# A fused attention and MLP kernel on one core: one decay moved ahead of two load issues, one weight load cut in two, four chunks' loads issued sooner and four stores later

## The chip, the core and the metric

The kernel runs on one core of a Trainium2 chip. The core has a matrix engine (TensorE, PE in the profile; its weight loads are listed as PEld), a vector engine (VectorE, DVE), a scalar engine (ScalarE, ACT), a general engine (GpSimd, POOL) and a queue engine that only issues transfers (SyncE, SP). Each runs its own list of instructions in order, and they meet through semaphores. Transfers between the device memory and the on-chip memory (DMA) are done by 16 DMA engines that all issuing engines share. In this kernel POOL issues all loads, which change float32 to bfloat16 on the way, and SP issues the stores and the transposing copies inside the on-chip memory.

The metric is device microseconds of one launch, as a median of several runs.

## The reference

Two stages follow each other. The first is a linear attention with decay, over 4 batches, 8 heads, 768 positions and head width 64, in blocks of 64 positions:

```python
for b in range(nb):
    qb, kb, vb = (q[:, :, sl], k[:, :, sl], v[:, :, sl])
    intra = einsum('bhic,bhjc->bhij', qb, kb) * Dmask
    intra = einsum('bhij,bhjd->bhid', intra, vb)
    inter = einsum('bhid,bhde->bhie', qb * lam_pow, kv_state)
    out[:, :, sl] = intra + inter
    kv_state = lam_block * kv_state + einsum('bhsd,bhse->bhde', kb * rev_pow, vb)
```

The second takes the 3072 tokens of width 512 that come out, and computes `gelu(x @ w_in) @ w_out` with an inner width of 2048 and the exact gelu.

## The kernel before, in words

**Tiling.** Positions go in chunks of 128 (two blocks of 64). Chunk n belongs to group n // 4 and batch n % 4, so a group is the same 128 positions of all four batches, 512 tokens, and there are 6 groups and 24 chunks. For each group the attention makes a tile x of 128 x 4 x 512, and the MLP of the group (`mlp`, L417 and on) follows. Its first product runs in 16 blocks of 128 inner columns (named a, b, m or l with the block's number; the gelu on ACT follows each), its second in 16 pieces p0 to p15. In group 0 piece p4k+i is the k-th quarter of w_out for tokens of batch i; in group 1 and later p4i+k is the k-th quarter for batch i.

**What a visit is.** While PE runs the MLP of one group it makes, between named blocks, the attention of the next. `visit(f, d)` (L335) gives PE the scores of chunk d (q times k) and its states (kv_ps: keys times decayed V), and between them the outputs of chunk f. It comes as some 32 matmul pairs of 64 x 64 that PE issues about 30 ns apart. Of a visit's pairs for d, the first eight are scores, the next four the states of the chunk's first block, and the last four those of its second block.

**What a chunk needs first.** Its k and q (two loads of 128 KB, L71), both transposed (`kqT`; by PE for chunks 0 to 7, from chunk 8 on by two transposing DMAs on SP, L245 and L246, asked for by `request`); its V with the decay (`vd`, `decay_v`, L266, one POOL multiplication); and its keys in a by-block arrangement (`k2`, `by_block`, L248), four copies of 64 x 256, of which two are made by POOL (by VectorE for chunks 4 and 7) and two by ACT or DVE. V comes for a whole group in four loads of 128 KB (`load_blocks`, L91).

**What sets the order.** It is written out by hand. `run_blocks` runs the blocks of an MLP and calls, ahead of the named ones, the steps in a table: the one after `run_blocks(mlp(0, 2)` for group 0 and `plan_of(g)` (L613) for the later ones. Each step only adds instructions to the ends of the engines' lists, so a step's name says when it stands in the program, and each engine works through its own list as its waits allow. `values(n)` is the decay and POOL's two key copies of chunk n, `keys(n)` the other two key copies, `fetch(n, m)` the loads of chunks n and m, with V of a group behind its first chunk.

**The loads at the start.** One call (L141) issues q, k and V of group 0, w_in, w_out, and k and q of chunks 4 to 7 with group 1's V. `i8-12` is blocks 8 to 12 of w_in in two DMAs (one for each half of the partitions), each 256 KB in bfloat16. The landings of POOL's loads are told by eight semaphores used in turn, so a load's issue waits until the load eight places before it has landed.

```python
    ask("k0 q0 k1 q1 k2 q2 k3 q3 v0 v2 i0-2 i2-4 i4-6 i6-8 i8-12 i12-16 "
        "o0-4 k4 q4 o4-8 V1 o8-12 k5 q5 o12-16 k6 q6 k7 q7")
```

**Behind them on POOL**, from `ahead_of_group_1` (L560): vd 4, vd 5, k8, the two key copies of chunk 5, q8, vd 6, the first quarter of group 2's V, vd 7, the second quarter, the key copies of chunk 6, the other two quarters, k9, q9. `visit(None, 4)` stands ahead of p8 of group 0, `visit(4, 5)` ahead of p11, `visit(5, 6)` ahead of p15. The third quarter of w_out (o8-12) is first read by p8.

**SP's list** holds the requests and the stores. The four outputs of group 0 are not stored when they are made: `store` (L451) keeps them in `held`, and `store_held` (L400) stores them at m0 of group 2's MLP. Output buffers (o_sb) come from nine in turn, so the tenth one waits for the first one's store. SP's transfers, too, have eight semaphores in turn.

Of the kernel before, what the change touches and what calls it, by code (L numbers as in the profile page):

```python
# [15 lines left out]
def kernel(  # L16
# [12 lines left out]
    B, H, S, D = q.shape  # L29
# [38 lines left out]
    def load(n, name):  # L68
        g, b = n // B, n % B
        t = raw[n, name] = qkv_pool.tile([128, H, D], BF16, tag=name, name=f"{name}_t", bufs=10)  # L70
        nc.gpsimd.dma_start(t, dram[name][b, :, g * C:(g + 1) * C, :].rearrange("h si d -> si h d"))  # L71
# [3 lines left out]
    def load_pairs(n, name):  # L75
        if (n, "kq") not in raw:
            raw[n, "kq"] = qkv_pool.tile([128, H, 2, D], BF16, tag="kq", name="kq_t", bufs=B)
        t = raw[n, "kq"][half("kq".index(name))]
        src = dram[name][n, :, :C, :].rearrange("h (p j) d -> p h (j d)", j=2)
        nc.gpsimd.dma_start(t.rearrange("p h j d -> p h (j d)"), src)  # L80

    def load_parity(n):

        t = qkv_pool.tile([128, 2 * H, D], BF16, tag="v", name="v_t", bufs=2)
        src = v[n:n + 2, :, :C, :].rearrange("b h (p j) d -> j p (b h) d", j=2)
        for j in range(2):
            nc.gpsimd.dma_start(t[half(j)], src[j])
        for i in range(2):
            raw[n + i, "v"] = t[:, i * H:(i + 1) * H, :]

    def load_blocks(g):  # L91

        t = raw["group", g] = qkv_pool.tile([128, 2, B * HP, D], BF16, tag="vg", name="vg_t", bufs=3)
        src = v.rearrange("b (hp hi) s d -> hi s (b hp) d", hi=2)
        for u in range(2):
            for hi in range(2):
                s = g * C + u * L
                nc.gpsimd.dma_start(t[half(hi), u], src[hi, s:s + L])  # L98
                yield
# [23 lines left out]
    def ask(items):  # L123

        for item in items.split():
            name, at = item[0], item[1:]
            if name in "kqv":
                n = int(at)
                if name == "v":
                    load_parity(n)  # L130
                elif n < B:
                    load_pairs(n, name)
                else:
                    load(n, name)
            elif name == "V":
                for _ in load_blocks(int(at)):
                    pass
            else:
                (load_w_in if name == "i" else load_w_out)(*(int(x) for x in at.split("-")))

    ask("k0 q0 k1 q1 k2 q2 k3 q3 v0 v2 i0-2 i2-4 i4-6 i6-8 i8-12 i12-16 "  # L141
        "o0-4 k4 q4 o4-8 V1 o8-12 k5 q5 o12-16 k6 q6 k7 q7")

    idle = consts.tile([128, 512], BF16)
    nc.vector.memset(idle, 0.0)  # L145
# [65 lines left out]
    def begin(n):  # L211
        c = live[n] = Chunk()
        c.n, c.g, c.b = n, n // B, n % B
        if c.g:
            c.q, c.k = (raw.pop((n, name)) for name in "qk")
        else:
            c.kq = raw.pop((n, "kq"))
        c.v = of_group(n) if c.g else raw.pop((n, "v"))
        c.kqT = work_pool.tile([128, 2, HP, C], BF16, tag="kqT", name="kqT", bufs=6)
        c.kT, c.qT = c.kqT[:, 0], c.kqT[:, 1]  # L220
        return c
# [22 lines left out]
    def dma_transposes(c):  # L244
        nc.sync.dma_start_transpose(out=c.kT, in_=c.k.rearrange("p h d -> p (h d)"))  # L245
        nc.sync.dma_start_transpose(out=c.qT, in_=c.q.rearrange("p h d -> p (h d)"))  # L246
# [16 lines left out]
    def of_group(n):  # L263
        return raw["group", n // B][:, :, n % B * HP:(n % B + 1) * HP, :]

    def decay_v(n):  # L266
        vd[n] = work_pool.tile([128, 2, HP, D], BF16, tag="vd", name="vd", bufs=6)
        nc.gpsimd.tensor_mul(vd[n], of_group(n), lam_vb)  # L268
# [131 lines left out]
    def store_held(some):  # L400
        for r, w, o_sb in held[some]:
            nc.sync.dma_start(out[r:r + C, w], o_sb)
# [147 lines left out]
    def request(*ns):  # L550
        for n in ns:
            dma_transposes(live[n])

    def same(n, eng):
        by_block(live[n], eng, None)
# [3 lines left out]

    def ahead_of_group_1():  # L560

        for n in range(B, 2 * B):
            begin(n)
        decay_v(4)
        decay_v(5)
        ask("k8")
        same(5, nc.gpsimd)
        ask("q8")
        decay_v(6)
        v_of_2 = load_blocks(2)  # L570
        next(v_of_2)
        decay_v(7)
        next(v_of_2)
        same(6, nc.gpsimd)
        for _ in v_of_2:
            pass
        ask("k9 q9")
        begin(8)
        begin(9)
# [17 lines left out]
    def values(n):  # L597
        decay_v(n)
        by_block(live[n], nc.gpsimd, None)

    def keys(n):
        by_block(live[n], None, nc.vector)

    def fetch(*ns):
        ns = [n for n in ns if n < NG * B]
        for n in ns:
            ask(f"k{n} q{n}")
            if n % B == 0 and n > 2 * B:
                ask(f"V{n // B}")
        for n in ns:  # L610
            begin(n)

    def plan_of(g):  # L613
        if g == 1:
            n = 2 * B
            return {
                "a0": [lambda: values(n), lambda: request(n + 1)],
                "a2": [lambda: visit(n - 2, n - 1, first=True)],
                "b2": [lambda: fetch(n + 2, n + 3)],
                "m5": [lambda: keys(n), lambda: request(n + 2, n + 3)],  # L620
                "m8": [lambda: values(n + 1), lambda: values(n + 2)],
                "m12": [lambda: fetch(n + 4, n + 5), lambda: request(n + 4, n + 5)],
                "m14": [lambda: visit(n - 1, n, first=True)],
                "l4": [lambda: values(n + 3), lambda: keys(n + 1)],
                "p1": [lambda: visit(n, n + 1)],
                "p2": [lambda: keys(n + 2), lambda: keys(n + 3)],
                "p5": [lambda: values(n + 4), lambda: fetch(n + 6, n + 7), lambda: values(n + 5)],
                "p7": [lambda: request(n + 6, n + 7)],
                "p8": [lambda: visit(n + 1, n + 2)],
                "p9": [lambda: keys(n + 4)],  # L630
                "p12": [lambda: visit(n + 2, n + 3)],
                "p13": [lambda: fetch(n + 8, n + 9)],
                "p15": [lambda: visit(n + 3, n + 4)],
            }
        if g == NG - 1:
            return {}
        n = (g + 1) * B
        if g == 2:
            return {
                "m0": [lambda: store_held(slice(0, B))],  # L640
                "m2": [lambda: keys(n + 1)],
                "m7": [lambda: visit(n, n + 1)],
                "m8": [lambda: values(n + 2), lambda: request(n + 4, n + 5)],
                "m10": [lambda: keys(n + 2), lambda: values(n + 3)],
                "m13": [lambda: keys(n + 3)],
                "m15": [lambda: visits([n + 1], [n + 2, n + 3], ["mo1"])],
                "p0": [lambda: fetch(n + 6, n + 7), lambda: values(n + 4)],
                "p2": [lambda: request(n + 6, n + 7), lambda: values(n + 5)],
                "p8": [lambda: keys(n + 4), lambda: keys(n + 5)],
                "p12": [lambda: visits([n + 2, n + 3], [n + 4, n + 5], ["mh", "mh"]), lambda: values(n + 6)],  # L650
            }

        def each(act, *ns):
            for n in ns:
                if n < NG * B:
                    act(n)

        return {
            "m0": [lambda: fetch(n + 4, n + 5), lambda: values(n + 3)],
            "m4": [lambda: keys(n + 2), lambda: keys(n + 3)],  # L660
            "m8": [lambda: each(request, n + 4, n + 5)],
            "m14": [lambda: visits([n, n + 1], [n + 2, n + 3], ["mo0", "mo1"]), lambda: each(values, n + 4)],
            "p0": [lambda: fetch(n + 6, n + 7), lambda: each(values, n + 5)],
            "p4": [lambda: each(request, n + 6, n + 7)],
            "p8": [lambda: each(keys, n + 4, n + 5)],
            "p12": [lambda: visits([n + 2, n + 3], [n + 4, n + 5], ["mh", "mh"]), lambda: each(values, n + 6)],
        }

    for g in range(1, NG):
        if g + 1 < NG:  # L670
            alloc_x(g + 1)
        run_blocks(mlp(g, 4, NK2) if g == 1 else mlp(g), plan_of(g))
# [29 lines left out]
```

## Time and profile before

| | us |
|---|---|
| timed runs | 210.36, 211.28, 212.76; median 211.28 |
| the profiled execution's own time | 210.23 |
| its span, first to last instruction | 208.2 |
| TensorE busy | 196.4 (94%) |
| GpSimd busy | 106.3 (51%) |
| VectorE, ScalarE busy | 88.7, 86.4 |
| DMA engines busy | over 0.9 of the span's first 29 of 40 slices, the first apart; little after |

All positions in time below are microseconds from the start of the span. Around the span lie 2.0 us more in the profiled execution's own time. In the list of an engine's instructions a line gives the start, the duration, engine, line of the source, operation and tiles, and in brackets the idle time before it and what ended that. "Landing" is the time from a DMA's issue to the semaphore that tells of its end. A wait is put down to what came last.

### The profile page before, as it was taken

To read this page: it belongs to the slowest core of one execution; us is meant where nothing else is said; L and a number is where in the kernel's file an instruction comes from. 1 tells how busy PE (TensorE), PEld (TensorE's weight loads), DVE (VectorE), ACT (ScalarE), POOL (GpSimd) and SP (SyncE) were. 2 spreads that over 40 slices of the span, in tenths; PEclk is the share of its full clock that TensorE was granted. 3 is DMA by queue.
4 is the path that set the end of the run, shared out by engine and by line. 5 is a ranking of instruction groups with operands and counts; after the bars stand their busy time and mean duration, and the time that the engine had idled before them with its cause. 6 is when DMAs were issued, how large, how long until landed. Compare 5 with 4: busy or idle time off the path is not lost.

```text
span 208.2 us, 5534 instructions
## 1 busy us (share of the span) xinstructions
PE 196.4 (94%) x2382; PEld 103.8 (50%) x2410; DVE 88.7 (43%) x188; ACT 86.4 (42%) x157; POOL 106.3 (51%) x150
## 2 busy tenths in 40 slices
PE   7789999799999999999998999999999999999992
PEld 4545345356758445445444445445445445444461
DVE  3869505167708669644934902946103202000000
ACT  5386561038675211556111465311565211665120
POOL 8979656699299949999649705950000000000000
PEclk9999999999999999999999999999999999999999
DMA  6999999999999999999999999994100021100121
GB/s 58 153 170 184 200 187 176 184 155 102 113 89 122 112 152 108 180 146 196 273 139 172 124 264 70 118 158 133 50 3 3 3 98 54 50 0 0 50 100 56
DMA packets 97337, 24.49 MB, mean 118 GB/s; under 512 B 88992, under 2 KB 94368, under 8 KB 97312
## 3 DMA queue, kind: packets, MB, share of 16 engines
q0 software_dynamic: 76160, 13.64, 89.4%
q1 hardware_dynamic: 21152, 10.50, 27.8%
q8 instruction: 19, 0.31, 0.7%
q14 instruction: 6, 0.05, 0.1%
HBM read 27.27 MB, written 6.29 MB: 161 GB/s over the span
## 4 chain that ended last, share of the span: by engine, by line
PE 44%; DMA 30%; POOL 22%; issue 2%; ACT 0%; POOLq 0%
PE h_ps L427 20%; PE o_ps L466 20%; DMA vg_t<-in_v_dram 12%; DMA q_t<-in_q_dram 8%; POOL vd L268 5%; DMA w_in_t<-in_moe_w_in_dram 4%; POOL q_t L71 3%; POOL vg_t L98 3%; DMA v_t<-in_v_dram 3%; POOL k_t L71 3%; POOL kq_t L80 3%; POOL k L255 3%; DMA kqT<-q_t 2%; POOL w_in_t L118 2%; PE o_ps L477 2%
## 5 line engine op out<-in xcount | busy, mean ns | idle before, releaser
L427 PE MATMUL h_ps<-x_t,w_in_t 128*128 128x512 bf16 (+3 forms) x399 | 81.9, 358 | 1.3 <-DMA w_in_t<-in_moe_w_in_dram 0.8
L466 PE MATMUL o_ps<-w_out_t,g_t 128*128 128x512 bf16 x352 | 80.9, 379 | 1.1 <-issue 0.5
L436 ACT ACTIVATE g_t<-h_ps 128x512 bf16<-128x512 f32 (+1 forms) x96 | 55.1, 580 | 32.0 <-PE h_ps L427 32.0
L427 PEld LDWEIGHTS <-w_in_t 128*128 128x128 bf16 x408 | 38.6, 98 | 41.4 <-issue 2.8
L466 PEld LDWEIGHTS <-g_t 128*128 128x128 bf16 x368 | 35.0, 98 | 40.3
L325 DVE TENSOR_TENSOR x_t<-o_ps,lam_o 128x512 bf16<-128x512 f32 x24 | 15.9, 688 | 60.8 <-PE o_ps L333 60.8
L455 ACT COPY o_sb<-o_ps 128x512 f32<-128x512 f32 (+1 forms) x25 | 14.2, 569 | 65.5 <-PE o_ps L466 60.1
L268 POOL TENSOR_TENSOR vd<-vg_t,lam_v 128x512 bf16<-128x512 bf16 x20 | 21.2, 1064 | 18.8 <-DMA vg_t<-in_v_dram 17.8
L71 POOL DMA_DIRECT2D q_t<-in_q_dram x20 | 18.1, 904 | 1.6 <-DMA vg_t<-in_v_dram 1.5
L71 POOL DMA_DIRECT2D k_t<-in_k_dram x20 | 18.2, 908 | 0.3 <-issue 0.2
L98 POOL DMA_DIRECT2D vg_t<-in_v_dram x20 | 16.4, 835 | 2.2 <-DMA w_in_t<-in_moe_w_in_dram 2.2
L255 POOL COPY k<-k_t 64x256 bf16<-64x256 bf16 x36 | 14.6, 405 | 3.6 <-DMA k_t<-in_k_dram 2.6
L279 DVE TENSOR_TENSOR sm<-sc_ps,dmask 128x512 bf16<-128x512 f32 x20 | 13.2, 681 | 5.4 <-PE sc_ps L333 5.4
L259 DVE COPY k<-k_t 64x256 bf16<-64x256 bf16 x34 | 13.1, 386 | 1.3 <-DMA k_t<-in_k_dram 0.8
L333 PEld LDWEIGHTS <-kqT 64*64 64x64 bf16 (+1 forms) x352 | 7.6, 107 | 7.5 <-issue 5.6
L333 PE MATMUL sc_ps<-kqT 64*64 64x64 bf16 (+1 forms) x352 | 10.2, 197 | 1.1 <-DMA kqT<-q_t 0.7
L333 PE MATMUL kv_ps<-vd,k 64*64 64x64 bf16 x288 | 8.0, 193 | 1.4 <-POOL vd L268 1.4
L504 PE MATMUL idle_ps<-idle 128*128 128x256 bf16 (+1 forms) x31 | 7.7, 391 | 1.3 <-DVE idle L145 1.2
L333 PE MATMUL o_ps<-sm,vg_t 64*64 64x64 bf16 x320 | 8.5, 193 | 0.0
L304 DVE TENSOR_TENSOR state<-t,lam_c 128x256 bf16<-128x256 f32 x16 | 8.1, 508 | 0.6
L118 POOL DMA_DIRECT2D w_in_t<-in_moe_w_in_dram x12 | 7.5, 667 | 1.2 <-DMA v_t<-in_v_dram 1.2
L298 DVE CAST mid<-t 128x256 bf16<-128x256 f32 x13 | 7.8, 597 | 0.4
(72 smaller groups left out, 132.2 us busy)
## 6 DMA issues: line engine op xcount, KB each, us to landing
out_dram<-o_sb SPq DMA_DIRECT2D x23, 256.0 KB, 4.8
k_t<-in_k_dram POOLq DMA_DIRECT2D x20, 128.0 KB, 7.1
q_t<-in_q_dram POOLq DMA_DIRECT2D x20, 128.0 KB, 7.2
vg_t<-in_v_dram POOLq DMA_DIRECT2D x20, 128.0 KB, 7.2
w_out_t<-in_moe_w_out_dram POOLq DMA_DIRECT2D x4, 512.0 KB, 11.2
w_in_t<-in_moe_w_in_dram POOLq DMA_DIRECT2D x8, 128.0 KB, 5.4
w_in_t<-in_moe_w_in_dram POOLq DMA_DIRECT2D x4, 256.0 KB, 7.4
kq_t<-in_k_dram POOLq DMA_DIRECT2D x4, 128.0 KB, 4.0
```

The source lines that it names most:

```text
L71: nc.gpsimd.dma_start(t, dram[name][b, :, g * C:(g + 1) * C, :].rearrange("h si d -> si h d"))
L98: nc.gpsimd.dma_start(t[half(hi), u], src[hi, s:s + L])
L255: same.tensor_copy(c.k2[half(hi), hi], k_r[half(hi), :, hi, :])
L259: copy(c.k2[half(hi), 1 - hi], k_r[half(1 - hi), :, hi, :])
L268: nc.gpsimd.tensor_mul(vd[n], of_group(n), lam_vb)
L279: nc.vector.tensor_mul(c.sm, c.sc, dmask)
L325: nc.vector.tensor_mul(xT[c.g][:, :, c.b * C:(c.b + 1) * C], c.o, lam_o)
L333: nc.tensor.matmul(out_, lhsT, rhs, start=start, stop=True, skip_group_check=True)
L427: nc.tensor.matmul(hs[kf][:, lo:up], w_in_t[:, ki, kf * 128:(kf + 1) * 128], x_t[:, ki, lo:up], start=(ki == 0 and lo == 0), stop=(ki == N ...
L436: nc.scalar.activation(g_t[:, kf, :up], hs[kf][:, :up], ACT.Gelu)
L455: nc.scalar.copy(o_sb, ps_)
L466: nc.tensor.matmul(om[io], g_t[:, kf, io * C:(io + 1) * C], w_out_t[:, kf, :], start=(kf == 0), stop=(kf == NK2 - 1))
```

## The change

There are four edits.

1. w_in's blocks 8 to 12 come in two loads of two blocks (`i8-10 i10-12`), so as four DMAs of 128 KB instead of two of 256 KB.
2. k7 and q7 leave the first list of loads. They are issued in `ahead_of_group_1`, k7 between the decays of chunks 4 and 5 and q7 behind the decay of chunk 5.
3. In group 1's MLP, the loads of chunks 14 and 15 stand ahead of the decay and key copies of chunk 12 instead of behind them, and the loads of chunks 16 and 17, with group 4's V, stand ahead of p11 instead of p13.
4. In group 2's MLP, the transposes of chunks 16 and 17 are asked for at m0 ahead of group 0's stores, instead of at m8 behind them.

On PE, VectorE and ScalarE the instructions and their order are the same in both kernels. POOL has two more load issues, and POOL and SP have the moved ones in other places.

```diff
-    ask("k0 q0 k1 q1 k2 q2 k3 q3 v0 v2 i0-2 i2-4 i4-6 i6-8 i8-12 i12-16 "
-        "o0-4 k4 q4 o4-8 V1 o8-12 k5 q5 o12-16 k6 q6 k7 q7")
+    ask("k0 q0 k1 q1 k2 q2 k3 q3 v0 v2 i0-2 i2-4 i4-6 i6-8 i8-10 i10-12 i12-16 "
+        "o0-4 k4 q4 o4-8 V1 o8-12 k5 q5 o12-16 k6 q6")
...
     def ahead_of_group_1():
 
+        decay_v(4)
+        ask("k7")
+        decay_v(5)
+        ask("q7")
         for n in range(B, 2 * B):
             begin(n)
-        decay_v(4)
-        decay_v(5)
         ask("k8")
         same(5, nc.gpsimd)
         ask("q8")
...
-                "p5": [lambda: values(n + 4), lambda: fetch(n + 6, n + 7), lambda: values(n + 5)],
+                "p5": [lambda: fetch(n + 6, n + 7), lambda: values(n + 4), lambda: values(n + 5)],
...
-                "p13": [lambda: fetch(n + 8, n + 9)],
+                "p11": [lambda: fetch(n + 8, n + 9)],
...
-                "m0": [lambda: store_held(slice(0, B))],
+                "m0": [lambda: request(n + 4, n + 5), lambda: store_held(slice(0, B))],
...
-                "m8": [lambda: values(n + 2), lambda: request(n + 4, n + 5)],
+                "m8": [lambda: values(n + 2)],
```

## The prediction

> **What bounds it now.** I read the busy shares first, then who TensorE (PE) waited for, then the order on GpSimd (POOL) and SyncE (SP) around those waits, and last the chain of waits. The page's first two lines
>
> ```profile
> span 208.2 us, 5534 instructions
> PE 196.4 (94%) x2382; PEld 103.8 (50%) x2410; DVE 88.7 (43%) x188; ACT 86.4 (42%) x157; POOL 106.3 (51%) x150
> ```
>
> and of the waits of PE's own (total us, times, longest us):
>
> ```profile
> PE kv_ps L333 <- POOL vd L268: 1.4, 1, 1.4
> ...
> PE h_ps L427 <- DMA w_in_t<-in_moe_w_in_dram: 0.8, 2, 0.4
> PE sc_ps L333 <- DMA kqT<-q_t: 0.7, 1, 0.7
> ```
>
> PE is busy for 94% at a granted clock of 1.0 in every slice, so no work can get faster; only waits can go. PE, DVE and ACT run the same instructions in the same order in both kernels; only POOL and SP differ. The change touches three waits: 0.40 us at 24.16 (the 0.8 is two waits; the other, at 16.67, is for blocks 0-2), 1.45 us at 41.12, 0.74 us at 112.00. Together 2.59 us, 1.2% of the span: the most it can win. What counts is what is late next, so I look at the stretch of POOL around the longest:
>
> ```profile
> 36.73 0.87 POOL L71 DMA_DIRECT2D k_t<-in_k_dram  x1 [0.18 <-issue]
> 39.09 0.87 POOL L71 DMA_DIRECT2D q_t<-in_q_dram  x1 [1.48 <-DMA vg_t<-in_v_dram]
> 40.03 2.04 POOL L268 TENSOR_TENSOR vd<-vg_t,lam_v 128x512 bf16<-128x512 bf16 x2
> 42.02 0.91 POOL L71 DMA_DIRECT2D k_t<-in_k_dram  x1
> 42.93 0.87 POOL L255 COPY k<-k_t 64x256 bf16<-64x256 bf16 x2
> ...
> 48.41 0.87 POOL L255 COPY k<-k_t 64x256 bf16<-64x256 bf16 x2
> ```
>
> Each load that POOL issues waits until the eighth load before it has landed. k7's issue (36.73) stands in the idle time before the last part of group 1's V lands (38.81, in the chain below); q7's stands right behind that landing, then the decays of chunks 4 and 5 (vd, 2.04 us for two), k8's issue, the two key copies of chunk 5, and so on without a gap to 52.6. From 39.09 on this queue is the path: whatever is put into it shifts all behind it.
>
> ```profile
> 26.87 11.94 DMA vg_t<-in_v_dram
> ...
> 90.85 16.94 DMA q_t<-in_q_dram
> ```
>
> These are pieces of the chain of waits (start, us): V's last part, then chunk 17's q, 16.94 us to land. Its transpose, issued at 107.81 and 4.15 us long, ends the 0.74 us wait at 112.00.
>
> **The change, part by part.**
>
> *w_in's blocks 8-12 in two loads.* Two more issues on POOL, 0.61 us each (the row of seven at 14.53 took 4.31). They are covered by POOL's later waits for landings (0.86, 1.07, 0.31, 1.71 us, from 22.2 on). In the trace the 256-column loads land 0.67 us apart, the 512-column ones 1.28 us, so four small ones take 2.68 us where two large took 2.56: +0.1 us for every later landing. PE comes to block 8 at 23.76 and now needs the first pair alone. That pair should land near 21.9 (20.60, the last small one's landing, + 2 x 0.67), and block 10 is reached at 25.5 with its pair at 23.3: **-0.40 us**. Blocks 12-16 land at 26.7, PE is there at 27.2.
>
> *Chunk 4's decay ahead of k7 and q7.* V's last part lands at 38.81 + 0.1, POOL starts 0.28 us later (as at 39.09): vd 4 runs 39.1-40.15 instead of 40.03-41.07. But PE's next need is the third quarter of w_out, issued at 29.39, 11.3 us to landing: 40.66, now 40.75. PE's part of kv (0.35 us) ends near 40.5, so w_out ends the stall, near 40.85, where before PE went on at 41.49: **-0.64 us, the 0.40 contained in it**, for PE arrives at either wait.
>
> *What this costs on POOL.* Behind the V landing stood one issue (q7) ahead of k8; now two do (k7, q7), because k7 has left the idle time. So everything from k8 on is one issue, 0.87 us, later, plus the 0.1. No queue hides it. The second copy of chunk 5's keys, needed by the fifth kv pair of the visit that PE starts at 44.63, ends at 44.75 instead of 43.80; PE would use it at 45.03 - 0.64 = 44.4 and so waits 0.35 us: 0.3 us of gain is left. The second copy of chunk 6's keys ends at 49.28 before (48.41 + 0.87) and at **50.2** after. PE uses it in the visit that starts at 49.31:
>
> ```profile
> 49.58 0.20 PE L333 MATMUL kv_ps<-vd,k 64*64 64x64 bf16 x2
> ...
> 49.71 0.20 PE L333 MATMUL kv_ps<-vd,k 64*64 64x64 bf16 x2
> ```
>
> These are the first kv pair and the fifth, which reads that copy. The slack before was 49.71 - 49.28 = 0.43 us; 0.95 us of delay takes it and 0.5 us more. PE leaves this visit **0.5 us later than before**, and the whole early gain is gone: -0.64 becomes +0.5. The size depends on V's landing alone: 0.9 us sooner would save all of it, 1 us later costs 1 us more.
>
> *Group 1.* POOL's next wait is for group 2's V (vd at 56.68 after 4.05 us idle). It covers part of the 0.95; I keep 0.3 us of shift (bounds 0 and 0.95). PE's visits there have several us of slack, except one: chunk 12's transposes, whose q is issued by SP at 73.27 and lands 8.2 us later, at 81.43, while PE starts that visit at 82.64. With PE 0.5 later the slack is 1.7 us; 0.3 is used.
>
> *Loads of chunks 14-17 sooner.* Chunks 14 and 15: four issues, 3.6 us, now ahead of chunk 12's decay (77.50) and in the 2.94 us that POOL idled for V there, so vd 12 and its copies end at 80.1, not 79.4; PE wants them at 82.9: nothing. Chunks 16 and 17 follow chunk 13's copies on POOL in both kernels (the move from p13 to p11 passes nothing there), but that queue has lost its idle time: they come about 2.9 us sooner (q17 at 88.0, not 90.85). But the four loads of 14 and 15 now run while chunk 12's transposes do. Bounds: 0 and 3.5 us (four landings 0.87 apart, as loads land at 45 to 50 us). I take 0.5, within the slack, since loads already in the queue (k13, q13) are those that it meets first. The Trainium skill (DMA: Bandwidth & Descriptors, Queues, rings and completion order) says that each DMA engine goes round-robin over its queues packet by packet; by that, the transposes would keep half of the turns and this wait would be 0; no view parts the two queues in time, so the trace does not decide it. The 8.2 us against the shortest landing of a transpose, 2.4 us, show how much a full load queue can cost in this trace, so I keep the upper end.
>
> *Group 0's stores behind the requests of 16 and 17.* SP before:
>
> ```profile
> 89.36 1.20 SPq L246 DMA_TRANSPOSE kqT<-q_t  x1
> 90.65 1.63 SPq L459 DMA_DIRECT2D out_dram<-o_sb  x3
> 92.33 2.07 SPq L402 DMA_DIRECT2D out_dram<-o_sb  x4
> 98.11 1.25 SPq L245 DMA_TRANSPOSE kqT<-k_t  x1
> ```
>
> Seven stores of 256 KB went out in 3.8 us, and q17, issued at 90.85 among them, took 16.94 us. Now three go ahead, and q17 has left 2.9 us sooner. At about 9 us it lands near 97, its transpose near 103 (4 to 8 us), 8 us ahead of PE: **-0.74 us**. The held stores wait behind it on SP until about 98 and land by 105; behind them stand the requests of 18 and 19, needed at 128. Their buffers are needed again at 107.25 (group 2's second o_sb copy of nine buffers): 2 us of slack, and PE has the other bank for 3.5 us more. Also chunk 15's transposes, which landed at 98.03 for a visit at 98.09, now have some us to spare.
>
> **Sum.** +0.5 (chunk 6's copy, early gains included) - 0.74 = **-0.25 us** on the profiled execution: 210.23 to 209.98 us. That execution is below all three timed runs (210.36, 211.28, 212.76; median 1.05 above it). What the slower ones lose is in no view; the least slack (0.06 us at 98.09, none at 112.00) lies where the change gives some, so I leave half of the 1.05 in: **210.5 us**, all cases below with the same 0.5.
>
> **Rivals.**
> *Early gain kept* (V lands sooner, or POOL's shift meets other idle time): -0.64 - 0.74 = -1.4, 209.35 us. For it: the key copies of 5 and 6 miss by only 0.3 and 0.5 us. Against: POOL has no idle time between 39.09 and 52.6. Chance 0.27; all three waits gone (-2.59, 208.15) is its end, against w_out's landing.
> *Slower: chunk 12's transposes pushed back* by the four loads issued at 74.6-78.2. Place: PE's visit at 82.6; it decides once the landing moves by over 1.7 us. At the upper end, 81.43 + 0.3 + 3.5 = 85.2 against 83.1: 2.1 us, -0.25 + 2.1 = +1.85, 212.6 us. For it: 8.2 us to land already. Against: k13 and q13 are ahead of them. Chance 0.18.
> *The late q17 stays late* (three stores and the transposes of 14 and 15 still stand around it): +0.5 alone, 211.2 us. Against it: 8 us of slack. Chance 0.1.
> Forecast: 0.45.
>
> **The numbers.** Within 1% is about what a measurement here can tell from no change (2.1 us, the spread of the three runs being 2.4). Forecast and the third rival lie within it; the first reaches over 1% only near its end, the second only with slow runs. Faster 0.2, same 0.67, slower 0.13. The range takes in the first rival (209.35, less 0.35 for part of its end) and most of the second: 209.0 to 212.4.
>
> **What would show it.** PE's waits after: none for w_in at block 8; kv for vd 4 at about 0.9 us and ended near 40.2, then a short one for w_out; new waits for POOL's key copy of 0.35 us at the visit of 5 and some 0.8 us at that of 6; none for kqT at the visit of 16 and 17. The first visit in group 1 starts 0.5 us later than 52.23. q17 lands within 10 us. I am wrong if there is no wait for POOL's copies, or if PE waits for chunk 12's transposes.

## The result and the profile after

The changed kernel is faster by about half a per cent: over 20 runs of each, a median of 209.12 us against 210.35 us, and a ratio of 0.9943 with a 95% interval of 0.992 to 0.9966. Slow executions, of which the only profiled one is that of e6_stores below (its granted clock was 0.5 for 3.4 us), are left out of every ratio and of every comparison of traces. The profiled execution took 209.00 us, with a span of 207.0 us, against 210.23 and 208.2. The forecast was 210.5 us and -0.25 us on the profiled execution; -1.23 us came. The sign is right and the size is not, so the question is which term carries the rest. Both medians lie 0.12 us above their profiled executions.

The page's first two lines and the list of PE's waits, of the kernel after:

```profile
span 207.0 us, 5564 instructions
PE 199.3 (96%) x2410; PEld 104.2 (50%) x2410; DVE 84.7 (41%) x188; ACT 86.5 (42%) x157; POOL 107.2 (52%) x152
```

```profile
PE t_ps L230 <- DMA kq_t<-in_k_dram: 1.6, 1, 1.6
PE idle_ps L504 <- DVE idle L145: 1.2, 1, 1.2
PE kv_ps L333 <- POOL k L255: 0.3, 1, 0.3
PE h_ps L427 <- DVE x_t L325: 0.2, 1, 0.2
```

PE's work is the same; its busy time is higher because the profile before lacks 28 matmul records (2382 of 2410). All three waits that the change aimed at are gone, also the one for chunk 4's decay, of which 0.9 us were to stay. The 1.6 us at 7.8 us lie in the start, which the change does not touch, among the transposes of the first chunks; PE reached group 0's MLP at 16.45 (16.67 before). The forecast new wait is there: PE waits for a key copy of POOL. It is larger than the list says, because half of it stands inside a matmul's duration. PE's order of instructions in that visit (start, us; in brackets the idle time before):

```profile
48.23 0.22 PE L333 MATMUL kv_ps<-vd,k 64*64 64x64 bf16 x2 [0.30 <-POOL k L255]
...
48.38 0.52 PE L333 MATMUL kv_ps<-vd,k 64*64 64x64 bf16 x2
48.69 0.22 PE L333 MATMUL o_ps<-kqT,mid 64*64 64x64 bf16 x2
```

The first kv pair waits for the first copy and the fifth, at 48.38, for the second: 0.52 us where others take 0.20. The visit lasts from 47.48 to 49.00, 1.5 us, where it took 0.7 before. POOL in the same stretch:

```profile
37.62 1.04 POOL L268 TENSOR_TENSOR vd<-vg_t,lam_v 128x512 bf16<-128x512 bf16 x1 [1.63 <-DMA vg_t<-in_v_dram]
38.60 0.91 POOL L71 DMA_DIRECT2D k_t<-in_k_dram  x1
39.53 1.06 POOL L268 TENSOR_TENSOR vd<-vg_t,lam_v 128x512 bf16<-128x512 bf16 x1
40.52 0.92 POOL L71 DMA_DIRECT2D q_t<-in_q_dram  x1
41.43 0.88 POOL L71 DMA_DIRECT2D k_t<-in_k_dram  x1
42.30 0.87 POOL L255 COPY k<-k_t 64x256 bf16<-64x256 bf16 x2
...
47.77 0.87 POOL L255 COPY k<-k_t 64x256 bf16<-64x256 bf16 x2
```

k7's issue stands behind V's landing, as foreseen, but V landed earlier than foreseen. The chain of waits has it (start, us):

```profile
19.22 7.42 DMA w_in_t<-in_moe_w_in_dram
...
26.93 10.52 DMA vg_t<-in_v_dram
```

V's last part landed at 37.44, not at 38.81. From the same load of w_in to this landing it took 10.8 us, against 12.2 in the profile before. PE began the first visit of group 1 at 51.22, 1.0 us sooner than before, where 0.5 us later had been forecast. Of this, 0.55 us is there when chunk 4's visit begins (38.69 against 39.24), mostly by the earlier start of the MLP and the missing wait at block 8; the rest comes behind V's landing. From the first visit of group 1 to the last matmul the two profiles differ by 0.16 us only (151.97 and 152.13), although the wait of 0.74 us is gone. So in this pair of executions nearly all of the gain is early. The end of SP's part:

```profile
87.78 1.52 SPq L459 DMA_DIRECT2D out_dram<-o_sb  x3
89.41 1.86 SPq L245 DMA_TRANSPOSE kqT<-k_t  x1
91.37 1.33 SPq L246 DMA_TRANSPOSE kqT<-q_t  x1
99.35 1.19 SPq L245 DMA_TRANSPOSE kqT<-k_t  x1
100.86 1.19 SPq L246 DMA_TRANSPOSE kqT<-q_t  x1
102.10 3.10 SPq L402 DMA_DIRECT2D out_dram<-o_sb  x4
```

Three stores go ahead, chunk 17's q lands at 100.84 and its transpose at 106.08, and the four held stores come behind. PE starts that visit at 109.95 without a wait.

Two explanations compete for the early part. **Theory A**: cutting w_in's load lets all that is queued behind it land sooner. **Theory B**: the landing of V varies between executions, and the profile before had a late one. For the late part the question is whether either the loads or the stores, or only both, end the wait (**C**: either; **D**: only both).

### The profile page after: what moved, and what is told of

Its sections match the earlier page's. It is cut to its first block, busy times and chain, and to the rows that moved or that the text cites. A ratio compares the mean times of both kernels' runs of the same rounds, so it can differ in the third digit from the quotient of the medians.

```text
span 207.0 us, 5564 instructions
## 1 busy us (share of the span) xinstructions
PE 199.3 (96%) x2410; PEld 104.2 (50%) x2410; DVE 84.7 (41%) x188; ACT 86.5 (42%) x157; POOL 107.2 (52%) x152
## 4 chain that ended last, share of the span: by engine, by line
PE 69%; DMA 12%; POOL 11%; DVE 4%; issue 1%; ACT 1%; POOLq 0%
PE h_ps L427 31%; PE o_ps L466 29%; DMA vg_t<-in_v_dram 5%; DMA w_in_t<-in_moe_w_in_dram 4%; DMA v_t<-in_v_dram 3%; POOL kq_t L80 3%; POOL w_in_t L118 2%; PE o_ps L333 2%; POOL vd L268 2%; PE sc_ps L333 2%; PE h_ps L444 2%; PE o_ps L477 2%; PE kv_ps L333 1%; ACT g_t L436 1%; DVE x_t L325 1%
## 5 line engine op out<-in xcount | busy, mean ns | idle before, releaser
L466 PE MATMUL o_ps<-w_out_t,g_t 128*128 128x512 bf16 x368 | 82.6, 379 | 0.0
L268 POOL TENSOR_TENSOR vd<-vg_t,lam_v 128x512 bf16<-128x512 bf16 x20 | 20.9, 1045 | 13.1 <-DMA vg_t<-in_v_dram 12.1
L279 DVE TENSOR_TENSOR sm<-sc_ps,dmask 128x512 bf16<-128x512 f32 x20 | 13.2, 681 | 5.4 <-PE sc_ps L333 5.4
L259 DVE COPY k<-k_t 64x256 bf16<-64x256 bf16 x34 | 12.0, 353 | 0.6
L504 PE MATMUL idle_ps<-idle 128*128 128x256 bf16 (+1 forms) x34 | 8.4, 382 | 1.2 <-DVE idle L145 1.2
L118 POOL DMA_DIRECT2D w_in_t<-in_moe_w_in_dram x14 | 8.7, 675 | 1.0 <-DMA v_t<-in_v_dram 1.0
L333 PE MATMUL kv_ps<-vd,k 64*64 64x64 bf16 x288 | 8.6, 194 | 0.5 <-POOL k L255 0.3
L304 DVE TENSOR_TENSOR state<-t,lam_c 128x256 bf16<-128x256 f32 x16 | 7.2, 449 | 0.5
L333 PEld LDWEIGHTS <-vg_t 64*64 64x64 bf16 x320 | 7.0, 107 | 0.0
```

Source lines behind the costliest of these rows:

```text
L118: nc.gpsimd.dma_start(w_in_t[half(1 - hi), :, f], w_in_r[hi, :, :, f])
L279: nc.vector.tensor_mul(c.sm, c.sc, dmask)
L333: nc.tensor.matmul(out_, lhsT, rhs, start=start, stop=True, skip_group_check=True)
L466: nc.tensor.matmul(om[io], g_t[:, kf, io * C:(io + 1) * C], w_out_t[:, kf, :], start=(kf == 0), stop=(kf == NK2 - 1))
```

## The experiments

Twelve runs were made, in three groups, each group on one chip beside runs of the kernel before. The last group repeats the changed kernel, e3 and e7. Edit 1 is the cut load, edit 2 the decay ahead of k7 and q7, edit 3 the loads of 14 to 17, edit 4 the stores behind the requests. "Stretch" is the time from PE's start of chunk 4's visit to its start of group 1's first visit (13.0 us in the profile before, 12.5 after); "V" is the time from the last landing of w_in to that of group 1's V (12.2 and 10.8 us); "late waits" are PE's waits for transposes at the visits near 98 and 112 us (0.74 and 0).

| kernel | edits | ratio, 95% interval | V | stretch | late waits |
|---|---|---|---|---|---|
| e1_split | 1 | 0.998 (0.9938 to 1.0021) | 11.2 | 12.0 | 0.20 |
| e2_decay | 2 | 0.997 (0.9932 to 1.0009) | 11.3 | 12.5 | 1.42 + 1.36 |
| e5_loads | 3 | 0.9947 (0.9902 to 0.9992) | 11.5 | 11.9 | 1.30 |
| e6_stores | 4 | 0.9925 (0.9881 to 0.997) | - | - | - |
| e3_loads_stores | 3, 4 | 0.9925 (0.9895 to 0.9955) | 10.4 | 11.5 | 0 |
| e11_loads_stores | 3, 4 | 0.9957 (0.9925 to 0.999) | 9.9 | 11.9 | 0 |
| e4_no_split | 2, 3, 4 | 0.9917 (0.9884 to 0.9949) | 10.2 | 12.0 | 0 |
| e8_no_decay | 1, 3, 4 | 0.9961 (0.9915 to 1.0007) | 11.0 | 12.4 | 0 |
| e10_after | all | 0.995 (0.9922 to 0.9978) | 11.8 | 12.8 | 0 |
| e7_k7_early | all, k7 early | 0.9951 (0.9909 to 0.9993) | 11.7 | 11.6 | 0.22 |
| e12_k7_early | all, k7 early | 0.9955 (0.9921 to 0.9988) | 9.8 | 11.4 | 0 |
| e9_best | 2, 3, 4, k7 early | 0.9932 (0.9893 to 0.997) | 11.4 | 11.5 | 0 |

**e1_split**, the first edit alone (the middle of the line):

```diff
-i4-6 i6-8 i8-12 i12-16
+i4-6 i6-8 i8-10 i10-12 i12-16
```

> The first edit alone (w_in's blocks 8 to 12 in two loads). Theory A: the split itself lets all that is queued behind it land sooner, as in the changed kernel's trace (the last part of group 1's V at 37.4 us instead of 38.8). Then V lands at 37.2 to 37.8 here too, PE has no wait for w_in at block 8, its wait for chunk 4's decay falls from 1.45 to about 0.5 us, the first visit of group 1 starts about 1.0 us sooner (51.2 instead of 52.2), and the time falls by what the later waits for transposes leave of it: ratio 0.995 to 1.000. Theory B (rival): V's landing varies from run to run by itself and the split does not move it. Then V lands near 38.8, only the 0.4 us at block 8 goes and comes back as a longer wait for the decay, ratio 1.000.

V took 11.2 us, in the range of A, and group 1's first visit started at 50.72. PE had no wait at block 8 and 0.41 us for the decay. By itself this would speak for A. The time did not move clear of noise.

**e2_decay**, the second edit alone:

```diff
-        "... o12-16 k6 q6 k7 q7")
+        "... o12-16 k6 q6")
...
+        decay_v(4)
+        ask("k7")
+        decay_v(5)
+        ask("q7")
         for n in range(B, 2 * B):
             begin(n)
-        decay_v(4)
-        decay_v(5)
```

> The second edit alone (k7 and q7 behind the decays of chunks 4 and 5). Theory A: without the split V's last part lands near 38.8 us, PE's wait for chunk 4's decay falls by 0.9 us, and the one load issue that POOL has more behind the landing makes PE wait 0.3 us for chunk 5's and 0.7 to 0.9 us for chunk 6's key copies: the first visit of group 1 starts 0.4 to 0.6 us later than 52.2, ratio 1.000 to 1.003. Theory B: V lands anywhere between 37.4 and 38.8; where it is early, the first visit of group 1 is up to 1 us sooner and the ratio below 0.998.

No split, and V took 11.3 us and landed at 37.03: A's number for this run was near 38.8. The waits for key copies are those of the changed kernel, and the visit of chunk 6 lasts 1.5 us again. PE's waits:

```profile
PE sc_ps L333 <- DMA kqT<-q_t: 2.8, 2, 1.4
...
PE kv_ps L333 <- POOL k L255: 0.3, 1, 0.3
```

The first line is what A and B both left out: without edits 3 and 4, this execution waited 1.42 us for chunk 15's transposes at 99.10 and 1.36 us for chunk 17's at 113.12, with q17 17.9 us to land. In the profile before these were 0 and 0.74 us.

**e3_loads_stores**, the third and fourth edit alone (the `lambda:` of each step left out):

```diff
-                "p5": [values(n + 4), fetch(n + 6, n + 7), values(n + 5)],
+                "p5": [fetch(n + 6, n + 7), values(n + 4), values(n + 5)],
-                "p13": [fetch(n + 8, n + 9)],
+                "p11": [fetch(n + 8, n + 9)],
-                "m0": [store_held(slice(0, B))],
+                "m0": [request(n + 4, n + 5), store_held(slice(0, B))],
-                "m8": [values(n + 2), request(n + 4, n + 5)],
+                "m8": [values(n + 2)],
```

> The third and fourth edit alone (loads of chunks 14 to 17 sooner, group 0's stores behind the requests of 16 and 17). Up to 82 us the trace is that of the kernel before (V at 38.8 by A; first visit of group 1 near 52.2). The wait of 0.74 us for chunk 17's transposes at 112 is gone; chunk 17's q lands before 102. Ratio 0.996 (-0.74 us) by both theories; if the loads pushed chunk 12's transposes back, PE waits at 82.6 and the ratio is 1.000 or more.

Ratio 0.9925, with an upper end of 0.9955: within the intervals, these two edits alone give what the whole change gives. There is no wait at 98 or at 112, q17 lands at 101.30. V took 10.4 us with no split, so the 37 us landing needs neither of the first two edits.

**e4_no_split**, edits 2, 3 and 4, is the changed kernel with `i8-12` in one load again.

> The changed kernel without the split (edits 2, 3 and 4). Theory A: V lands near 38.8, first visit of group 1 0.4 to 0.6 us late, the late wait gone: -0.25 us against the kernel before, ratio 0.999, the 1 us that the changed kernel has more is the split's. Theory B: ratio 0.994 to 0.996, as the changed kernel, with V before 38 us.

0.9917 with an upper end of 0.9949, and V after 10.2 us: not A's 0.999, and below B's 0.994 too. V landed at 38.30, not before 38, but w_in's last part had landed 1.5 us later than in the profile before. Over the thirteen traces that are compared V takes 9.8 to 11.8 us with the split (six, mean 11.0) and 9.9 to 12.2 without it (seven, mean 11.0); it lands at 37.5 and 37.7 us on average. **Theory A falls.** The 12.2 us of the profile before is the longest of the thirteen.

**e5_loads** and **e6_stores** are e3's edit in two halves: the first two pairs of lines above in the one, the last two in the other.

> The third edit alone (loads of chunks 14 to 17 sooner; the seven stores stay ahead of the requests of 16 and 17). Theory C: either edit ends the late wait by itself. Then chunk 17's q, issued near 86, lands before 104, its transpose before 109, and PE has no wait at 98 or 110 to 113; ratio 0.993 to 0.996. Theory D: only both together do it, since seven stores still go out among the loads. Then q17 lands at 104 or later, PE waits up to 1 us for chunk 17's transposes, and the ratio is 0.997 to 1.000.

> The fourth edit alone (group 0's stores behind the requests of 16 and 17; loads where they were). Theory C: q17, issued near 90 with three stores beside it instead of seven, lands before 102, no wait at 110 to 113; what is left is the small slack of chunk 15's transposes at 98 (0 to 1.4 us of wait, as in the runs without the third edit); ratio 0.994 to 0.998. Theory D: q17 lands after 104, the wait stays at 0.2 to 1.4 us, ratio 0.998 to 1.000.

In e5_loads SP has the seven stores together again:

```profile
89.82 1.59 SPq L459 DMA_DIRECT2D out_dram<-o_sb  x3
91.47 3.17 SPq L402 DMA_DIRECT2D out_dram<-o_sb  x4
97.02 1.28 SPq L245 DMA_TRANSPOSE kqT<-k_t  x1
...
107.08 1.19 SPq L246 DMA_TRANSPOSE kqT<-q_t  x1
```

q17 was issued at 87.87, 3 us sooner than in the kernel before, and landed at 107.06, 19.2 us later. PE waited 1.30 us at 111.51; chunk 15's transposes landed at 96.94, just as PE began that visit. So in this execution earlier loads did not end the wait at 112, which is D; but the ratio of 0.9947 is C's, not D's. For the stores alone 0.9925 is faster than both theories' numbers. In the one trace of e6_stores q17 landed at 106.65, and PE waited 2.15 us for chunk 15's transposes at 99.47 and none for chunk 17's, to whose visit it came late, at 112.95. Both intervals reach from 0.988 or 0.990 to 0.997 or 0.999 and do not part the two halves, nor either half from both. That each half alone leaves a late wait is thus seen in one trace each; how the gain in time divides between the two stays open.

**e7_k7_early**, the changed kernel with k7's issue back in the time when POOL waits for V:

```diff
-        "... o12-16 k6 q6")
+        "... o12-16 k6 q6 k7")
...
         decay_v(4)
-        ask("k7")
-        decay_v(5)
         ask("q7")
+        decay_v(5)
```

> The changed kernel with k7's issue back in POOL's idle time before V lands (list: vd 4, q7, vd 5, k8), so that one issue less stands behind V's landing. If that issue is what PE pays for at the visit of chunk 6, the wait for its key copies (0.3 + 0.12 us, and a visit of 1.5 us instead of 0.7) is gone, from the start of chunk 4's visit to the first visit of group 1 it takes 11.5 to 11.7 us instead of 12.0 to 12.5, and the ratio is 0.3 us better than the changed kernel's: 0.9925. If the cost is elsewhere (ACT's or DVE's copies), the stretch stays at 12.0 to 12.5 us and the ratio at 0.994.

The wait for POOL's key copies is gone from PE's list, and the stretch is 11.6 us: the issue behind V's landing is what PE paid for. The ratio, 0.9951, is not the 0.9925 that was expected, and no better than the changed kernel's. The trace shows 0.42 us of wait for chunk 12's transposes (81.26) and 0.22 us for chunk 15's.

**e8_no_decay**, edits 1, 3 and 4.

> The changed kernel without the second edit (edits 1, 3 and 4). If that edit costs more than it gives in most executions, the stretch from chunk 4's visit to the first visit of group 1 is 11.5 to 12.0 us when V's last part lands 11 us or less after w_in's last, and the ratio is 0.992 to 0.993, better than the changed kernel's 0.9943. If it gives what was forecast for it, PE waits 0.4 us or more for chunk 4's decay here, and the ratio is 0.995 or more.

V took 11.0 us, and PE still waited 0.85 us for chunk 4's decay. Its stretch of 12.4 us lies beside the changed kernel's 12.5: in such an execution the second edit gives about what it costs. The signs of the second expectation came (a wait of 0.4 us or more, a ratio of 0.995 or more) and the first one's stretch did not, but the ratio's interval holds both numbers.

The last four ran on one chip: **e9_best** (the changed kernel with `i8-12` in one load and k7 early), **e10_after** (the changed kernel), **e11_loads_stores** and **e12_k7_early** (e3 and e7 again).

> Edits 3 and 4, and chunk 4's decay ahead of q7 alone, with k7's issue left in POOL's idle time; w_in's load not cut. If the split brings nothing beside 0.4 us that is lost again at the wait for chunk 4's decay, and the extra issue behind V is what the second edit costs, this is the fastest: no PE wait for POOL's key copies, chunk 4's visit to the first visit of group 1 in 11.5 to 11.7 us, ratio 0.991 to 0.993. If the split's 0.4 us stays, it is 0.2% behind the version with the split of the same call.

> The changed kernel once more, beside the three others on one chip. Ratio 0.994 as measured; PE waits for the key copies of chunk 6 again (0.3 to 0.4 us in all, in a visit of some 1.5 us), 12.0 to 12.5 us from chunk 4's visit to the first visit of group 1, no wait at 98 and at 110 to 113 us. If its first profile was a chance, the wait for the key copies is missing here.

> Edits 3 and 4 alone once more. If they are the whole gain, ratio 0.992 to 0.995 and not slower than the changed kernel beside it; from chunk 4's visit to the first visit of group 1 11.4 to 13.0 us, by where V's last part lands. If the first two edits bring 0.6 us, as the kernel before would need at its late V landing, this one is 0.3% behind the changed kernel.

> The changed kernel with k7's issue in POOL's idle time once more, beside the changed kernel on one chip. No wait for the key copies of chunks 5 and 6, 11.5 to 11.7 us from chunk 4's visit to the first visit of group 1, and 0.3 to 0.6 us less than the changed kernel (ratio 0.991 to 0.993). If that issue does not count, the same time as the changed kernel.

Medians 208.27, 208.63, 208.79 and 208.79 us, and all four intervals overlap: the first two edits, in either form, make no difference in time that these runs can tell. e11_loads_stores is 0.1% behind the changed kernel, not 0.3%, and e12_k7_early is 0.16 us slower than it, where 0.3 to 0.6 us faster was expected. Over all groups, the ratios of kernels with edits 3 and 4 are 0.9917 to 0.9957 without the split (four, mean 0.9933) and 0.9943 to 0.9961 with it (five, mean 0.9952); whether the split costs some tenths is open. The traces do tell the mechanism. e10_after waits 0.3 us for the key copies again, and this time 0.3 us for w_out's third quarter and 0.25 us for chunk 12's transposes too. Its stretch is 12.8 us. In e9_best, POOL has k7's issue ahead of the decay and nothing of the kind is left on PE; the stretch is 11.5 us:

```profile
37.11 0.87 POOL L71 DMA_DIRECT2D k_t<-in_k_dram  x1 [0.48 <-DMA vg_t<-in_v_dram]
38.08 1.04 POOL L268 TENSOR_TENSOR vd<-vg_t,lam_v 128x512 bf16<-128x512 bf16 x1
39.06 0.91 POOL L71 DMA_DIRECT2D q_t<-in_q_dram  x1
39.99 1.05 POOL L268 TENSOR_TENSOR vd<-vg_t,lam_v 128x512 bf16<-128x512 bf16 x1
```

```profile
PE idle_ps L504 <- DVE idle L145: 1.2, 1, 1.2
PE o_ps L333 <- DMA v_t<-in_v_dram: 1.0, 2, 0.6
PE t_ps L230 <- DMA kq_t<-in_k_dram: 0.3, 1, 0.3
```

These last are all of PE's listed waits in e9_best, and all lie before 17 us. It has the lowest median of its group, 0.36 us below the changed kernel beside it, which the intervals do not confirm.

## Why the prediction was right, and where its sizes were off

Of the 1.4 us between the forecast of 210.5 and the median of 209.12, 1.0 is the change (-0.25 forecast, -1.23 measured) and 0.4 the level. That the time came as near as it did is in part luck: the range had been drawn out for the first rival, and the forecast's early loss of 0.5 us did not come.

**Edit 1, w_in.** Right in kind: no trace with the split has a wait at block 8, and blocks 8 to 10 and 10 to 12 landed at 21.66 and 23.00 (21.9 and 23.3 forecast). The size of 0.40 us was one execution's; over the traces without the split that wait is 0 to 0.42 us. That the split costs later landings nothing to speak of (+0.1 us forecast) fits V's mean landings, 37.5 us with it and 37.7 without.

**Chunk 4's decay.** The step that failed is "V's last part lands at 38.81 + 0.1". I took one landing as a property of the kernel. In the changed kernel it came at 37.44 and 37.45, so the decay ended at 38.66, not 40.15, PE had no wait for it, and the 1.45 us that the edit was to cut was the extreme of a wait that is 0 to 0.9 us in the other traces with the old order. The forecast named this dependence ("0.9 us sooner would save all of it"), and the rival *early gain kept* rested on it: its time of 209.35 us is nearer the 209.12 measured than the forecast's 210.5. Its condition came true in the pair of profiles, where V landed 1.4 us sooner and 1.0 us of the gain is early. But V lands as early without the first two edits (36.82 us in e3_loads_stores), and the runs show no difference in time by them: that early gain is a draw of the landing, not the change's.

**What it costs on POOL.** Right in kind, and near in size. One more issue stands behind the landing. The visit of chunk 5 took 1.0 us instead of 0.7 (0.35 forecast), that of chunk 6 1.5 instead of 0.7 (0.8 forecast); e2_decay and e10_after have the 1.5 us too, and e4_no_split, where V landed sooner against PE (1.7 us ahead of chunk 4's visit, not 1.0 to 1.3), has 1.1. With k7's issue ahead of the decay it is 0.75 to 0.87. The stretch is 12.0 to 12.8 us in the four with the second edit as it was made, 11.4 to 11.6 with k7 early, and 11.5 to 13.0 with the old order; the means are 12.5, 11.5 and 12.1. So in most executions the second edit gives nothing or loses some tenths. That the forecast's 0.35 and 0.8 us came so near is partly luck: POOL's copies and PE were both some 1.5 us earlier than forecast, which leaves the difference as it was.

**Chunk 12's transposes.** Rightly left in the background. q12's transpose took 6.4 to 9.1 us to land with the loads of 14 and 15 sooner (ten traces, mean 7.7), and 7.9 to 8.2 with the old order (three): on average it was not pushed back. This speaks against the 3.5 us that I kept as the upper end. In the mean it fits the rule of the Trainium skill that the forecast cites (DMA: Bandwidth & Descriptors, Queues, rings and completion order), of queues that take turns packet by packet. A wait of 0.25 to 0.42 us at that visit was seen in two traces, far from 2.1; one of them is e10_after, so the forecast's own sign of being wrong there came in one of two traces of the changed kernel.

**Chunks 14 to 17 and the stores.** Right in kind, mis-sized twice. First, q17 took 14.8 us to land (16.0 in e10_after), not about 9: three stores and the transposes still stand around it. The slack at the visit was 3.9 us, and 1.8 in e10_after, not 8. The third rival was nearer than its chance of 0.1 said. Second, and this is where the gain of the medians seems to lie, the 0.74 us was again one execution's. In the four traces without both edits (the kernel before, e1, e2 and e5, so four kernels) the late waits are 0.74, 0.20, 2.78 and 1.30 us, 1.25 on average; in eight of the nine with both they are 0, in the ninth 0.22. From group 1's first visit to the last matmul it takes 152.1, 151.9, 154.7 and 153.1 us in the four, 152.9 on average, and 151.2 to 152.9, 151.7 on average, in the nine. That is 1.2 us, about the measured gain. Four traces that differ by 2.8 us are few for such a mean; what shows that edits 3 and 4 bring a gain of this size by themselves are the ratios of e3_loads_stores and e11_loads_stores, whose whole intervals lie below 1, while those of edit 1 and of edit 2 alone hold 1.

**The level.** Half of the 1.05 us between the profiled execution and the median was left in, on the guess that the slower runs lose the other half where the change gives slack. Most of the 1.05 was not the kernel's: the median that was shown, 211.28 of three runs, lay 0.9 us above the median of twenty, and with twenty runs the median is 0.12 us above the profiled execution before and after.

## What to carry to other kernels

A wait that ends on a DMA landing is a draw, not a constant: before its size goes into a sum, ask what the same landing does in other executions, and price an edit that gives slack by the average wait over several executions, not by the one in the profile (here 1.25 us, over four kernels, against 0.74). When an instruction is pulled ahead of load issues on the same queue, look which of them stood in idle time: moving only those behind the landing's wait cost PE no listed wait for the key copies here, while an issue taken out of an idle stretch shifted everything behind it. And a store burst is better placed behind the requests that feed the next visit when the loads can't be kept away from it.

## What the runs showed of the hardware that was not expected

Loads among stores land late: q17 (128 KB) took 16.9 to 19.2 us in the four traces where all seven stores go out ahead of the requests of 16 and 17, and 13.2 to 16.6 in the nine where three do, while loads of the same size took 7 us at the median and, in the profile before, at most 11.9 at the start, where there are no stores. The forecast said that no view parts the two queues in time, but the view of DMA in a window does. In the kernel before, from 96 to 100 us (packets, MB, share of 16 engines; the hardware queue holds SP's transfers, the software queue POOL's loads):

```profile
q1 hardware_dynamic: 501, 0.91, 92.9%
q0 software_dynamic: 501, 0.06, 24.3%
```

The two queues moved the same number of packets, and the loads about a fifteenth of the bytes. Elsewhere the counts differ (2155 against 4487 from 73.3 to 81.4 us, while q12's transpose was under way), so equal turns are shown for this stretch and not in general.

The cast of `mid` on VectorE took 0.29 us at its shortest, and 1.13 and 1.01 us when POOL's multiplication ran beside it. In the kernel before, the view of VectorE in a short window, and then that of POOL:

```profile
77.55 1.13 DVE L298 CAST mid<-t 128x256 bf16<-128x256 f32 x1
```

```profile
77.50 1.04 POOL L268 TENSOR_TENSOR vd<-vg_t,lam_v 128x512 bf16<-128x512 bf16 x1 [2.94 <-DMA vg_t<-in_v_dram]
```

The cast started 0.05 us after the multiplication and ended 0.14 us after it. In that profile all six casts that start during a multiplication end 0.14 to 0.15 us after its end (they are 0.68 to 1.13 us long). After the change the same happens at 76.54 (1.01 us beside a multiplication from 76.37 to 77.41). The chain of waits there runs through VectorE from 74.9 to 83.5 us, and PE takes 1.92 us from the start of chunk 12's visit to the next block of the MLP, 1.55 before; how much of the difference is the cast's is not shown. The Trainium skill (SBUF — State Buffer, SBUF: two separate sides) says that VectorE in some modes and GpSimd share a port pair which one holds for a whole instruction; both lines agree with that.
